# Weights loaded into the place they are converted in, a conversion in four stages, and y stored from one tile: a change to a fused attention and two-layer kernel

## The chip, the cores and the metric

The kernel runs on one core of a Trainium2 chip. The metric is the device time of one execution in microseconds, the median over runs. Before the change it is 770.56 us (three runs, 769.83 to 771.4).

## What is computed

Three layers follow each other, all in float32 (only the weights arrive as float64):

```python
# 1. attention with local masks: 4 batches, 8 heads, 576 positions, head size 64
scores = where(mask, q @ k.T / 8, -1e9)        # plain window 32, or dilated by 4
x = softmax(scores) @ v                        # -> 2304 tokens x 512
# 2. first feed-forward layer
h = x @ w_in                                   # 512 -> 2048
y = (h - tanh(h)) @ w_out                      # 2048 -> 512
# 3. second feed-forward layer
h = y @ w_in2                                  # 512 -> 1024
u = h * softmax(h)
out = ((u - mean(u)) / sqrt(var(u) + 1e-6) * g_ln) @ w_out2   # 1024 -> 512
```

## The kernel before

**Weights.** Every weight matrix is cut into pieces of 128 x 512 values: 16 of `w_in`, 16 of `w_out`, 8 each of `w_in2` and `w_out2`. A piece comes from HBM as raw float64 words, 512 KB (`w_load`, on SP's queue), and is turned into two float32r halves, high and low, by five or six instructions: ScalarE scales the upper word (`a`), VectorE takes the sign (`and`), merges exponent and mantissa in two `scalar_tensor_tensor` steps, ScalarE writes the high half (`hi`, a cast), VectorE subtracts for the low half (`lo`). `w_step` does one such step for several pieces at once: in its stages a piece is new, then merged, then split. In the kernel before, `hi` and the `lo` that reads it stand first in the same call (`w_parts`). Raw words lie in a pool of three buffers, the two halves in pools `wi` and `wo`.

**Phase 1, attention of the first 384 tokens.** Eight units (a pair of heads and a pair of query blocks each) go through a loop of eleven rounds. A round r does the score matmuls of unit r (`qk_f32`), the value matmuls of unit r-3 (`pv_pe`), the transposes of unit r-2 (`tr_pe`), one `w_step` (in rounds 1 to 10), and then on VectorE the masked reduction of unit r (line 163), on ScalarE its four exponentials, on VectorE the reciprocal of the sums of unit r-1, and on GpSimd the normalisation (line 205). At a round's end `load_unit(r + 3)` issues two loads on SP's queue: `qkr` (two buffers) and `v` (four buffers).

**Phase 2, first layer and the rest of the attention.** 96 steps s (6 groups of 384 tokens x 16 pieces) run, each of two slots: `mm1(s)`, twelve matmuls of `h`, and `mm2(s - 5)`, twelve matmuls that add to the four PSUM tiles of `y`. Between them stand the pieces of the 40 other attention units, placed by slot (`plan`), and in the first 42 slots the rest of the `w_step` calls, at a pace set by `WA / WB`. From unit 22 the scores use float32r halves made by `prep_unit`. At a group's last step `mm2` copies the four tiles to SBUF (`ys`) and stores them to HBM (`y_dr`), two at a time through one buffer. In the last group (s = 80 on) the 16 pieces of the second layer are converted, one `w_step` a step, and `y` is read back (`yr`).

**Phase 3, second layer.** 18 blocks of 128 tokens, with `mm3`, `trz` and `mm4`.

Each engine works through its instructions in program order, and so does SP's queue of DMA issues: a wait there holds back all that is behind it. A buffer that is handed out again makes its new writer wait for all readers of the old content, also where those stand later in the program.

Of the kernel before, what the change touches and what calls it, by code (L numbers as in the profile page):

```python
# [7 lines left out]
F32 = mybir.dt.float32  # L8
F32R = mybir.dt.float32r
I32 = mybir.dt.int32  # L10
AF = mybir.ActivationFunctionType
ALU = mybir.AluOpType
# [3 lines left out]
B, H, S, D = 4, 8, 576, 64  # L16
# [3 lines left out]
G = 384  # L20
NG = NTOK // G
NQ, NK = 96, 128
NU = 8
QC, KC = 4 * NQ, 4 * NK
KD = DM // 128
NF = FF // 128
NF2 = FF2 // 128
# [1 line left out]
NT = NTOK // TT  # L29
YT = 256  # L30
LAG = 5
WA, WB = 24, 40
SW = range(1, 11)
W0 = 11

# [2 lines left out]
def tile_kernel(ctx: ExitStack, tc: tile.TileContext, qk, vw, cst, w_in, w_out, w_in2, w_out2, g_ln, out):  # L38
    nc = tc.nc
    ctx.enter_context(tc.manual_schedule())  # L40

    const = ctx.enter_context(tc.tile_pool(name="const", bufs=1, side="left"))
    wi_p = ctx.enter_context(tc.tile_pool(name="wi", bufs=NF, side="left"))
    wo_p = tc.alloc_tile_pool(name="wo", bufs=NF, side="left")
    raw_p = tc.alloc_tile_pool(name="raw", bufs=3, side="left")
    qs_p = None
    g_p = ctx.enter_context(tc.tile_pool(name="g", bufs=2, side="right"))
    x_p = ctx.enter_context(tc.tile_pool(name="x", bufs=2, side="right"))
    at_p = tc.alloc_tile_pool(name="at", bufs=2, side="right")
# [19 lines left out]

    wq, wld, wa, wf = [], [], [], []

    def w_load():
        if wq:
            lst, c, pool, src, tag, nm = wq.pop(0)
            raw = raw_p.tile([128, 1024], I32, tag="raw", name="raw_" + nm)
            nc.sync.dma_start(out=raw, in_=src)
            wld.append((lst, c, pool, tag, nm, raw.rearrange("p (n t) -> p n t", t=2)))

    def w_parts():
        if wf:
            lst, c, pool, tag, nm, f = wf.pop(0)
            w = pool.tile([128, 2, 512], F32R, tag=tag, name=nm)
            nc.scalar.copy(out=w[:, 0], in_=f)
            nc.vector.tensor_tensor(out=w[:, 1], in0=f, in1=w[:, 0].bitcast(F32), op=ALU.subtract)
            lst[c] = w

    def w_step():

        w_parts()
        new = wld.pop(0) if wld else None
        if new:
            lst, c, pool, tag, nm, r = new
            a = raw_p.tile([128, 512], F32, tag="wa", name="wa_" + nm, bufs=2)
            y = raw_p.tile([128, 512], I32, tag="wy", name="wy_" + nm, bufs=3)
            nc.scalar.activation(out=a, in_=r[:, :, 1].bitcast(F32), func=AF.Copy, scale=2.0 ** -112)
            nc.vector.tensor_scalar(out=y, in0=r[:, :, 1], scalar1=-2 ** 31, scalar2=None, op0=ALU.bitwise_and)
        if wa:
            *e, ao, yo = wa.pop(0)  # L100
            nc.vector.scalar_tensor_tensor(out=yo, in0=ao.bitcast(I32), scalar=3, in1=yo,
                                           op0=ALU.logical_shift_left, op1=ALU.bitwise_or)
            wf.append((*e, yo.bitcast(F32)))
        if new:
            nc.vector.scalar_tensor_tensor(out=y, in0=r[:, :, 0], scalar=29, in1=y,  # L105
                                           op0=ALU.logical_shift_right, op1=ALU.bitwise_or)
            wa.append((lst, c, pool, tag, nm, a, y))
        w_load()

    wi, wo = [None] * NF, [None] * NF  # L110

    for c in range(NF + LAG):
        if c < NF:
            wq.append((wi, c, wi_p, w_in[c], "wi", f"wi{c}"))
        if c >= LAG:
            wq.append((wo, c - LAG, wo_p, w_out[c - LAG], "wo", f"wo{c - LAG}"))

# [3 lines left out]
    def load_unit(u):  # L123
        if u < NU * NG:
            r = at_p.tile([128, QC + KC], F32, tag="qkr", name=f"qkr{u}")
            n = 64 if u < NFU else 128
            nc.sync.dma_start(out=r[:n], in_=qk[u, :n])
            v = at_p.tile([NK, 2, 2, D], F32, tag="v", name=f"v{u}", bufs=4)
            nc.sync.dma_start(out=v.rearrange("p b h d -> p (b h d)"), in_=vw[u])
            un[u] = dict(r=r, v=v)  # L130

    def prep_unit(u):
        if not NFU <= u < NU * NG:
            return []
        r = un[u]["r"]
        s = qs_p.tile([128, QC + 2 * KC], F32R, tag="qks", name=f"qks{u}")
        un[u]["s"] = s
        return [
            lambda: nc.vector.tensor_copy(out=s[:, 0:QC + KC], in_=r),
            lambda: nc.vector.tensor_tensor(out=s[64:128, 0:QC], in0=r[64:128, 0:QC],  # L140
                                            in1=s[64:128, 0:QC].bitcast(F32), op=ALU.subtract),
            lambda: nc.vector.tensor_tensor(out=s[:, QC + KC:], in0=r[:, QC:],
                                            in1=s[:, QC:QC + KC].bitcast(F32), op=ALU.subtract),
        ]
# [106 lines left out]
    load_unit(1)  # L251
    w_load()
    load_unit(2)
    w_load()
    back = None
    for r in range(NU + 3):
        t = qk_f32(r, st_ps, "qk") if r < NU else None
# [26 lines left out]
    ghl, yb = {}, {}  # L284
# [3 lines left out]
    def at(slot, fn):  # L288
        later.setdefault(slot, []).append(fn)
# [28 lines left out]
    def mm2(s):  # L318
        g, c = divmod(s, NF)
        gs = ghl.pop(s)  # L320
        if c == 0:
            yb[g] = [y_ps.tile([128, 512], F32, tag=f"y{m}", name=f"y{g}_{m}")[:, 0:G] for m in range(KD)]
        for m in range(KD):
            for i, (a, b) in enumerate(((0, 0), (0, 1), (1, 0))):
                nc.tensor.matmul(yb[g][m], wo[c][:, a, m * 128:(m + 1) * 128], gs[:, b],  # L325
                                 start=(c == 0 and i == 0), stop=(c == NF - 1 and i == 2))
        if c == NF - 1:
            for i in range(0, KD, 2):
                ys = g_p.tile([128, 2, G], F32, tag="ys", name=f"ys{g}_{i}", bufs=1)
                nc.vector.tensor_copy(out=ys[:, 0], in_=yb[g][i])  # L330
                nc.scalar.copy(out=ys[:, 1], in_=yb[g][i + 1])
                nc.scalar.dma_start(out=y_dr[:, i:i + 2, g * G:(g + 1) * G], in_=ys)

    u0, u1 = NU, NU * NG
    preps = []
# [4 lines left out]
    def plan():  # L340


        ready = 0
        for u in range(u0, u1 + 2):
            p = 4 * u - 41 if u >= 2 * NU else (2, 6, 8, 12, 14, 16, 18, 20)[u - u0]
            q = p + 2 if u >= 2 * NU or u < u0 + 4 else p + 1
            if u < u1:
                at(p, lambda u=u: preps.extend(prep_unit(u + 1)))
                for i in range(3):
                    at(p + i, lambda: preps.pop(0)() if preps else None)  # L350
                if u < NFU:
                    piece(p, lambda u=u: qk_f32(u, a_ps, "at"))
                    at(p + 1, lambda u=u: sm_exp(u))
                    at(p + 2, lambda u=u: sm_norm(u))
                else:
                    piece(p, lambda u=u: qk_half(u, 0, a_ps, "at"))
                    at(p + 2, lambda u=u: sm_exp(u, (0, 1)))
                    piece(p + 1, lambda u=u: qk_half(u, 1, a_ps, "at"))
                    at(p + 3, lambda u=u: sm_exp(u, (2, 3)))
                    at(p + 4, lambda u=u: sm_norm(u))  # L360
                at(p + 1, lambda u=u: load_unit(u + 2))
            if u0 <= u - 1 < u1:
                piece(q, lambda u=u: tr_pe(u - 1, a_ps, "at"))
            if u0 <= u - 2 < u1:
                piece(q + 1, lambda u=u: pv_pe(u - 2, a_ps, "at"))
# [3 lines left out]

    NS = NG * NF  # L370
    w2i, w2o = [None] * (2 * KD), [None] * NF2
    wq2 = [(w2i, 2 * k + n, wi_p, w_in2[k, n], "wi", f"w2i{2 * k + n}") for k in range(KD) for n in range(2)]
    wq2 += [(w2o, j, wi_p, w_out2[j], "wi", f"w2o{j}") for j in range(NF2)]

    yt, y_raw = {}, {}

# [17 lines left out]
    slot = 0  # L394
    done = [len(SW)]
    for s in range(NS + LAG):
        if s == NF + LAG:
            assert not (wq or wld or wa or wf)
            raw_p.release()
            qs_p = tc.alloc_tile_pool(name="qs", bufs=2, side="left", reuse_waits="tile")  # L400
        if s == NS - NF:
            assert not todo and not later and not (wq or wld or wa or wf), (todo, later)
            a_ps.release()
            at_p.release()
            qs_p.release()
            raw_p = tc.alloc_tile_pool(name="raw2", bufs=2, side="left", reuse_waits="tile")
            h2a = tc.alloc_tile_pool(name="h2a", bufs=1, space=PSUM, side="right", reuse_waits="tile")
            p2 = tc.alloc_tile_pool(name="p2", bufs=2, side="right", reuse_waits="tile")
            wq.extend(wq2)
            w_load()  # L410
            w_load()
# [31 lines left out]
            load_y(2)  # L443
    for fn in nxt:
        fn()
    while wq or wld or wa or wf:
        w_step()


    raw_p.release()  # L450
    wo_p.release()
    h_ps.release()
    y_ps.release()
# [182 lines left out]
```

## Time and profile before

| | |
|---|---|
| time, median of 3 runs | 770.56 us |
| profiled execution, its own time | 771.82 us |
| its span, first to last instruction | 770.0 us |
| TensorE busy | 729.4 us, 95% |
| VectorE, ScalarE, GpSimd busy | 470.0, 367.1, 132.3 us |
| mean granted TensorE clock | 0.989 |

Times inside the profile are counted from the span's start. A busy TensorE is not one at its peak: the same twelve matmuls take 2.1 to 4.2 us in different places. A bracket behind an instruction of the timeline tells how long its engine had been idle before it, and what ended that.

### The profile page before, as it was taken

Reading aid. Unit: us, or ns where it says so; the run is one execution under the profiler, and the core shown is the slowest. Engines: PE = TensorE matmul, PEld = TensorE weight load, DVE = VectorE, ACT = ScalarE, POOL = GpSimd, SP = SyncE. Lnnn points to the kernel's source line nnn. Section 1 sums busy time; section 2 is a strip of 40 time slices with the busy share of each in tenths; the row PEclk is TensorE's granted clock in tenths of the full one; section 3 lists DMA queues with packets and bytes.
Section 4 is the critical chain, followed back from the end, with each engine's and each line's share of the span. In section 5 each row is a group of like instructions: output and inputs, shape, how many; then the busy total and the mean of one; then the engine's idle time right before and its main releaser. Section 6 shows DMA issues by size and latency. Waiting matters only on the chain.

```text
span 770.0 us, 11751 instructions
## 1 busy us (share of the span) xinstructions
PE 729.4 (95%) x4168; PEld 657.8 (85%) x4168; DVE 470.0 (61%) x1297; ACT 367.1 (48%) x1015; POOL 132.3 (17%) x187
## 2 busy tenths in 40 slices
PE   5658899999999999999999999799999999999998
PEld 4547789999999899989998999799888888888885
DVE  4688788746665766666666535498365555555453
ACT  4656666644443544444444434345145544445454
POOL 1210322111111111111111100010133123231210
PEclk9999899999999999999999999899999999999999
DMA  7565354222222222121212102434201011110001
GB/s 188 180 215 154 110 187 162 92 70 77 63 62 78 88 63 63 62 89 55 64 61 94 63 1 82 155 133 138 68 1 56 29 40 56 42 54 28 14 28 42
DMA packets 30283, 63.62 MB, mean 83 GB/s; under 512 B 3088, under 2 KB 16912, under 8 KB 30224
## 3 DMA queue, kind: packets, MB, share of 16 engines
q1 hardware_dynamic: 26960, 58.15, 23.6%
q10 hardware_dynamic: 3264, 4.72, 1.7%
q8 instruction: 33, 0.54, 0.3%
q14 instruction: 26, 0.21, 0.1%
HBM read 53.42 MB, written 9.44 MB: 82 GB/s over the span
## 4 chain that ended last, share of the span: by engine, by line
PE 88%; DMA 4%; DVE 3%; ACT 2%; issue 1%; POOL 1%; SPq 0%; ACTq 0%; POOLq 0%; DVEq 0%
PE y L325 27%; PE h L298 25%; PE po L529 13%; PE h L467 13%; PE pv L233 3%; PE zt L510 2%; DMA raw_wi<-in_w_in_dram 2%; PE qkp L158 2%; PE tp L212 2%; PE qkp L178 2%; ACT p L198 1%; DMA y_dr<-ys 1%; POOL p L205 1%; DVE wy_wi L105 1%; DMA raw_wo<-in_w_out_dram 0%
## 5 line engine op out<-in xcount | busy, mean ns | idle before, releaser
L298 PE MATMUL h<-x,wi 128*128 128x384 f32 x1152 | 225.3, 346 | 3.3 <-DVE x L244 2.0
L325 PE MATMUL y<-gs,wo 128*128 128x384 f32 x1152 | 222.6, 343 | 4.3 <-DVE ys L330 4.3
L325 PEld LDWEIGHTS y<-gs,wo 128*128 128x128 f32 x1152 | 199.9, 190 | 9.4 <-DVE ys L330 4.6
L298 PEld LDWEIGHTS h<-x,wi 128*128 128x128 f32 x1152 | 202.0, 193 | 5.5 <-DVE x L244 2.3
L205 POOL TENSOR_TENSOR p<-p,rs 96x512 f32<-96x512 f32 x48 | 77.9, 1623 | 368.0 <-DVE rs L204 315.3
L306 ACT ACTIVATE t<-h 128x384 f32<-128x384 f32 x96 | 46.9, 489 | 125.3 <-PE h L298 119.3
L467 PE MATMUL h<-w2i,yt 128*128 128x512 f32 x432 | 104.9, 397 | 0.0
L529 PE MATMUL po<-w2o,z 128*128 128x512 f32 x432 | 104.1, 396 | 0.1
L529 PEld LDWEIGHTS po<-w2o,z 128*128 128x128 f32 x432 | 80.7, 188 | 20.4 <-ACT z L518 1.9
L518 ACT ACTIVATE z<-zt,gl_sb 128x128 fp32r<-128x128 f32 x144 | 51.0, 367 | 96.9 <-PE zt L510 48.6
L467 PEld LDWEIGHTS h<-w2i,yt 128*128 128x128 f32 x432 | 79.7, 187 | 18.4
L198 ACT ACTIVATE p<-p,nm 96x128 f32<-96x128 f32 x192 | 75.0, 393 | 36.3 <-DVE nm L163 36.3
L519 DVE SCALAR_TENSOR_TENSOR z<-zt,gl_sb,z 128x128 fp32r<-128x128 f32 x144 | 48.9, 350 | 69.2 <-ACT z L518 69.2
L312 ACT CAST gs<-t 128x384 fp32r<-128x384 f32 x96 | 49.1, 511 | 54.0 <-DVE t L309 53.7
L244 DVE TENSOR_TENSOR x<-pv,x 128x192 fp32r<-128x192 f32 x48 | 20.5, 428 | 77.1 <-ACT x L243 77.1
L309 DVE TENSOR_TENSOR t<-h,t 128x384 f32<-128x384 f32 x96 | 52.9, 551 | 23.0 <-ACT t L306 22.9
L315 DVE TENSOR_TENSOR gs<-t,gs 128x384 fp32r<-128x384 f32 x96 | 56.1, 585 | 9.8 <-ACT gs L312 9.7
L233 PE MATMUL pv<-pt,v 128*64 128x96 f32 x384 | 29.7, 281 | 15.7 <-ACT pt L218 9.1
L233 PEld LDWEIGHTS pv<-pt,v 128*64 128x64 f32 x384 | 19.8, 151 | 28.6 <-issue 12.4
L158 PE MATMUL qkp<-qkr 64*96 64x128 f32 x176 | 31.6, 334 | 8.2 <-DMA qkr<-in_qk_dram 7.6
L387 POOL TENSOR_TENSOR yt<-yr,yt 128x1024 fp32r<-128x1024 f32 x9 | 21.9, 2430 | 93.9 <-DMA raw_w2o<-in_w_out_dram 62.3
L158 PEld LDWEIGHTS qkp<-qkr 64*96 64x96 f32 x176 | 25.9, 201 | 13.0 <-DMA qkr<-in_qk_dram 6.9
(68 smaller groups left out, 708.2 us busy)
## 6 DMA issues: line engine op xcount, KB each, us to landing
qkr<-in_qk_dram SPq DMA_DIRECT2D x26, 448.0 KB, 3.4
raw_wi<-in_w_in_dram SPq DMA_DIRECT2D x16, 512.0 KB, 4.5
raw_wo<-in_w_out_dram SPq DMA_DIRECT2D x16, 512.0 KB, 4.2
v<-in_vw_dram SPq DMA_DIRECT2D x48, 128.0 KB, 2.1
qkr<-in_qk_dram SPq DMA_DIRECT2D x22, 224.0 KB, 4.3
y_dr<-ys ACTq DMA_DIRECT2D x12, 384.0 KB, 2.4
yr<-y_dr SPq DMA_DIRECT2D x9, 512.0 KB, 4.1
out_dram<-o SPq DMA_DIRECT2D x18, 256.0 KB, 2.0
```

The costliest lines, as they stand in the source:

```text
L158: nc.tensor.matmul(ps[:, b], d["r"][:64, b * NQ:(b + 1) * NQ], d["r"][:64, QC + b * NK:QC + (b + 1) * NK], start=True, stop=True)
L198: nc.scalar.activation(out=d["p"][:, b], in_=d["p"][:, b], func=AF.Exp, scale=-1.0, bias=d["nm"][:, b:b + 1], accum_out=d["sm"][:, b:b + 1])
L205: nc.gpsimd.tensor_tensor(out=d["p"], in0=d["p"], in1=d["rs"].unsqueeze(2).to_broadcast([NQ, 4, NK]), op=ALU.mult)
L233: nc.tensor.matmul(ps[64 * h:64 * h + 64, b * NQ:(b + 1) * NQ], d["v"][:, b, h], d["pt"][:, (2 * h + b) * NQ:(2 * h + b + 1) * NQ], start= ...
L298: nc.tensor.matmul(ps, w[:, a, k * 128:(k + 1) * 128], xt[g, k][:, b], start=(n == 0), stop=(n == 3 * KD - 1))
L309: nc.vector.tensor_tensor(out=t, in0=ps, in1=t, op=ALU.subtract)
L312: nc.scalar.copy(out=gs[:, 0], in_=t)
L315: nc.vector.tensor_tensor(out=gs[:, 1], in0=t, in1=gs[:, 0].bitcast(F32), op=ALU.subtract)
L325: nc.tensor.matmul(yb[g][m], wo[c][:, a, m * 128:(m + 1) * 128], gs[:, b], start=(c == 0 and i == 0), stop=(c == NF - 1 and i == 2))
L467: nc.tensor.matmul(ps[:, n * 512:(n + 1) * 512], y[:, a, k, o:o + TT], w2i[2 * k + n][:, b], start=(q == 0), stop=(q == 3 * KD - 1))
L518: nc.scalar.activation(out=z[:, 0, c], in_=pp[n][:, j], func=AF.Copy, scale=gc)
L529: nc.tensor.matmul(po, z[:, a, j], w2o[j][:, b], start=(q == 0), stop=(q == 3 * NF2 - 1))
```

## The change

- `raw` is allocated under the tag of the piece's final place, one tag for each of the 16 places of `wi` and of `wo`; the three raw buffers are gone. The second layer's 16 pieces take the places wi0 to wi15, so their load waits for the last matmul that reads the place.
- Four raw pieces are asked for ahead of the rounds, where there were two.
- `w_step` has one more stage: `lo` of a piece comes one call after its `hi`, and stands first; `a` and `and` of the new piece come before the `hi`. `WA` is 26 for 24.
- `v` has five buffers for four. The float32r scores' tile `qks` has one buffer for two, in another pool, and its three preparing instructions come two slots later (the copy) and two and one later (the subtractions).
- `ys` holds all four tiles; VectorE copies tiles 0 and 2, ScalarE 1 and 3, and one DMA of 768 KB stores them.

```diff
-WA, WB = 24, 40
+WA, WB = 26, 40
...
-    wi_p = ctx.enter_context(tc.tile_pool(name="wi", bufs=NF, side="left"))
-    wo_p = tc.alloc_tile_pool(name="wo", bufs=NF, side="left")
-    raw_p = tc.alloc_tile_pool(name="raw", bufs=3, side="left")
+    cv_p = ctx.enter_context(tc.tile_pool(name="cv", bufs=2, side="left"))
+    wi_p = ctx.enter_context(tc.tile_pool(name="wi", bufs=1, side="left"))
+    wo_p = tc.alloc_tile_pool(name="wo", bufs=1, side="left")
...
-            raw = raw_p.tile([128, 1024], I32, tag="raw", name="raw_" + nm)
+            raw = pool.tile([128, 1024], I32, tag=tag, name="raw_" + nm)
...
-    def w_parts():
+    def w_step():
+
+        if wh:
+            lst, c, w, f = wh.pop(0)
+            nc.vector.tensor_tensor(out=w[:, 1], in0=f, in1=w[:, 0].bitcast(F32), op=ALU.subtract)
+            lst[c] = w
+        new = wld.pop(0) if wld else None
+        if new:
+            *e, r = new
+            a = cv_p.tile([128, 512], F32, tag="wa", name="wa_" + e[-1])
+            y = cv_p.tile([128, 512], I32, tag="wy", name="wy_" + e[-1], bufs=4)
+            nc.scalar.activation(out=a, in_=r[:, :, 1].bitcast(F32), func=AF.Copy, scale=2.0 ** -112)
+            nc.vector.tensor_scalar(out=y, in0=r[:, :, 1], scalar1=-2 ** 31, scalar2=None, op0=ALU.bitwise_and)
         if wf:
             lst, c, pool, tag, nm, f = wf.pop(0)
             w = pool.tile([128, 2, 512], F32R, tag=tag, name=nm)
             nc.scalar.copy(out=w[:, 0], in_=f)
-            nc.vector.tensor_tensor(out=w[:, 1], in0=f, in1=w[:, 0].bitcast(F32), op=ALU.subtract)
-            lst[c] = w
...
+            wh.append((lst, c, w, f))
...
-            v = at_p.tile([NK, 2, 2, D], F32, tag="v", name=f"v{u}", bufs=4)
+            v = at_p.tile([NK, 2, 2, D], F32, tag="v", name=f"v{u}", bufs=5)
...
-        s = qs_p.tile([128, QC + 2 * KC], F32R, tag="qks", name=f"qks{u}")
+        s = at_p.tile([128, QC + 2 * KC], F32R, tag="qks", name=f"qks{u}", bufs=1)
...
     load_unit(2)
-    w_load()
+    for _ in range(3):
+        w_load()
...
-            for i in range(0, KD, 2):
-                ys = g_p.tile([128, 2, G], F32, tag="ys", name=f"ys{g}_{i}", bufs=1)
-                nc.vector.tensor_copy(out=ys[:, 0], in_=yb[g][i])
-                nc.scalar.copy(out=ys[:, 1], in_=yb[g][i + 1])
-                nc.scalar.dma_start(out=y_dr[:, i:i + 2, g * G:(g + 1) * G], in_=ys)
+            ys = g_p.tile([128, KD, G], F32, tag="ys", name=f"ys{g}", bufs=1)
+            for m in range(KD):
+                if m % 2 == 0:
+                    nc.vector.tensor_copy(out=ys[:, m], in_=yb[g][m])
+                else:
+                    nc.scalar.copy(out=ys[:, m], in_=yb[g][m])
+            nc.scalar.dma_start(out=y_dr[:, :, g * G:(g + 1) * G], in_=ys)
...
-                at(p, lambda u=u: preps.extend(prep_unit(u + 1)))
-                for i in range(3):
+                at(p + 2, lambda u=u: preps.extend(prep_unit(u + 1)))
+                for i in (2, 3, 3):
...
-    wq2 = [(w2i, 2 * k + n, wi_p, w_in2[k, n], "wi", f"w2i{2 * k + n}") for k in range(KD) for n in range(2)]
-    wq2 += [(w2o, j, wi_p, w_out2[j], "wi", f"w2o{j}") for j in range(NF2)]
+    wq2 = [(w2i, 2 * k + n, wi_p, w_in2[k, n], f"wi{2 * k + n}", f"w2i{2 * k + n}")
+           for k in range(KD) for n in range(2)]
+    wq2 += [(w2o, j, wi_p, w_out2[j], f"wi{2 * KD + j}", f"w2o{j}") for j in range(NF2)]
```

## Rows read from the trace of the kernel before

**Rows 1.** The page's slices: TensorE's busy tenths in 40 equal parts of the span.

```profile
PE   5658899999999999999999999799999999999998
```

**Rows 2.** Chain that ended last, first 60 us: start us, us, what.

```profile
18.18 4.99 DMA raw_wi<-in_w_in_dram
...
52.88 4.22 PE h L298 x12
```

**Rows 3.** Timeline of rounds 6 and 7: start, us, engine, line, what, [idle before <-releaser].

```profile
32.13 0.62 ACT L85 CAST wi<-wy_wi 128x512 fp32r<-128x512 f32 x1
...
32.78 0.69 DVE L86 TENSOR_TENSOR wi<-wy_wi,wi 128x512 fp32r<-128x512 f32 x1 [1.47 <-ACT wi L85]
...
35.00 0.28 DVE L163 CUSTOM_DVE_ANT_0 p<-qkp,cst_sb 96x128 f32<-96x128 f32 x1
...
36.30 0.17 DVE L204 RECIPROCAL rs<-rs 96x4 f32<-96x4 f32 x1
...
36.65 1.04 POOL L205 TENSOR_TENSOR p<-p,rs 96x512 f32<-96x512 f32 x1 [4.13 <-ACT p L198]
...
40.25 0.28 DVE L163 CUSTOM_DVE_ANT_0 p<-qkp,cst_sb 96x128 f32<-96x128 f32 x1
```

**Rows 4.** Timeline of SP's issues, 5 to 20 us.

```profile
7.56 0.44 SPq L78 DMA_DIRECT2D raw_wi<-in_w_in_dram  x1
9.45 0.47 SPq L127 DMA_DIRECT2D qkr<-in_qk_dram  x1
...
17.75 0.34 SPq L129 DMA_DIRECT2D v<-in_vw_dram  x1
```

**Rows 5.** SP queue's waits, first 53 us: total us, times, longest.

```profile
SPq L129 <- PE pv L233: 21.4, 6, 4.1
```

**Rows 6.** The qkr load issued at 9.45, issue to landing.

```profile
DMA to landing us min/median/max: 4.9/4.9/4.9
```

**Rows 7.** Busy time by stretch: span, engines' busy us, PEclk, DMA share, GB/s.

```profile
2.00:16.00 14.00, 8.39 (x35) 7.19 (x36) 5.87 (x33) 5.92 (x25) 1.32 (x2) 1.00 0.95 249
16.00:52.88 36.88, 21.48 (x128) 16.02 (x126) 26.50 (x93) 24.56 (x77) 7.24 (x7) 1.00 0.56 182
...
80.30:110.25 29.95, 29.81 (x189) 26.70 (x189) 23.83 (x78) 19.46 (x61) 7.77 (x4) 0.92 0.42 139
```

**Rows 8.** VectorE's line 86, 57 to 77 us: busy, mean ns, idle before it.

```profile
L86 DVE TENSOR_TENSOR wi<-wy_wi,wi 128x512 fp32r<-128x512 f32 x2 | 1.4, 694 | 2.4 <-ACT wi L85 2.4
```

**Rows 9.** Timeline around the longest wait of TensorE in phase 2's start.

```profile
76.25 0.66 DVE L86 TENSOR_TENSOR wo<-wy_wo,wo 128x512 fp32r<-128x512 f32 x1
...
76.49 2.85 POOL L205 TENSOR_TENSOR p<-p,rs 96x512 f32<-96x512 f32 x1 [8.21 <-DVE rs L204]
...
79.39 0.90 PE L212 MATMUL tp<-cst_sb,p 96*128 96x96 f32 x4 [4.25 <-POOL p L205]
```

**Rows 10.** Timeline of the second group's store.

```profile
251.09 0.56 DVE L330 COPY ys<-y 128x384 f32<-128x384 f32 x1 [3.04 <-DMA y_dr<-ys]
```

**Rows 11.** Chain behind that store.

```profile
251.48 1.26 issue
```

**Rows 12.** Chain around the fifth group's store.

```profile
480.61 2.08 PE h L298 x12
...
484.27 7.14 DMA y_dr<-ys
...
498.25 2.09 PE y L325 x12
```

**Rows 13.** Landing of the eight raw_w2i loads.

```profile
DMA to landing us min/median/max: 3.0/3.2/4.4
```

**Rows 14.** Timeline in the last group: two of ScalarE's instructions of one step.

```profile
470.69 0.66 ACT L97 ACTIVATE wa_w2i<-raw_w2i 128x512 f32<-128x512 f32 x1
...
474.46 0.49 ACT L306 ACTIVATE t<-h 128x384 f32<-128x384 f32 x1 [2.53 <-PE h L298]
```

**Rows 15.** Timeline of phase 2: VectorE's idle time ahead of line 244.

```profile
242.49 0.36 DVE L244 TENSOR_TENSOR x<-pv,x 128x192 fp32r<-128x192 f32 x1 [2.80 <-ACT x L243]
```

More of the change, by code (lines that the diff above doesn't have):

```diff
@@ L42, in tile_kernel @@
     const = ctx.enter_context(tc.tile_pool(name="const", bufs=1, side="left"))
-    wi_p = ctx.enter_context(tc.tile_pool(name="wi", bufs=NF, side="left"))
-    wo_p = tc.alloc_tile_pool(name="wo", bufs=NF, side="left")
-    raw_p = tc.alloc_tile_pool(name="raw", bufs=3, side="left")
-    qs_p = None
+    cv_p = ctx.enter_context(tc.tile_pool(name="cv", bufs=2, side="left"))
+    wi_p = ctx.enter_context(tc.tile_pool(name="wi", bufs=1, side="left"))
+    wo_p = tc.alloc_tile_pool(name="wo", bufs=1, side="left")
     g_p = ctx.enter_context(tc.tile_pool(name="g", bufs=2, side="right"))
@@ L66, in tile_kernel @@
     gl_sb = const.tile([128, NF2], F32, name="gl_sb")
-    wq, wld, wa, wf = [], [], [], []
+    wq, wld, wa, wf, wh = [], [], [], [], []
     def w_load():
@@ L85, in w_parts @@
             nc.scalar.copy(out=w[:, 0], in_=f)
-            nc.vector.tensor_tensor(out=w[:, 1], in0=f, in1=w[:, 0].bitcast(F32), op=ALU.subtract)
-            lst[c] = w
[L89 to L98, printed above, removed]
+            wh.append((lst, c, w, f))
         if wa:
-            *e, ao, yo = wa.pop(0)
+            *eo, ao, yo = wa.pop(0)
             nc.vector.scalar_tensor_tensor(out=yo, in0=ao.bitcast(I32), scalar=3, in1=yo,
                                            op0=ALU.logical_shift_left, op1=ALU.bitwise_or)
-            wf.append((*e, yo.bitcast(F32)))
+            wf.append((*eo, yo.bitcast(F32)))
         if new:
@@ L106, in w_step @@
                                            op0=ALU.logical_shift_right, op1=ALU.bitwise_or)
-            wa.append((lst, c, pool, tag, nm, a, y))
+            wa.append((*e, a, y))
         w_load()
@@ L113, in tile_kernel @@
         if c < NF:
-            wq.append((wi, c, wi_p, w_in[c], "wi", f"wi{c}"))
+            wq.append((wi, c, wi_p, w_in[c], f"wi{c}", f"wi{c}"))
         if c >= LAG:
-            wq.append((wo, c - LAG, wo_p, w_out[c - LAG], "wo", f"wo{c - LAG}"))
+            wq.append((wo, c - LAG, wo_p, w_out[c - LAG], f"wo{c - LAG}", f"wo{c - LAG}"))
     xt, un = {}, {}
@@ L396, in tile_kernel @@
     for s in range(NS + LAG):
[L397 to L400, printed above, removed]
         if s == NS - NF:
-            assert not todo and not later and not (wq or wld or wa or wf), (todo, later)
+            assert not todo and not later and not (wq or wld or wa or wf or wh), (todo, later)
             a_ps.release()
             at_p.release()
-            qs_p.release()
-            raw_p = tc.alloc_tile_pool(name="raw2", bufs=2, side="left", reuse_waits="tile")
             h2a = tc.alloc_tile_pool(name="h2a", bufs=1, space=PSUM, side="right", reuse_waits="tile")
@@ L445, in tile_kernel @@
         fn()
-    while wq or wld or wa or wf:
+    while wq or wld or wa or wf or wh:
         w_step()
-    raw_p.release()
     wo_p.release()
```

## The prediction

> **What bounds the kernel now.** I read the page's slices first [rows 1]: TensorE is at 5 to 8 tenths in the first five slices (96 us) and at 9 from then on, with one dip near 490 us. So the time can shrink in the start, at the dip, and in waits too short for a slice; between them TensorE sets the pace, and faster work on other engines buys nothing.
>
> The chain of waits through the start shows what sets the pace there. It passes through loads of raw weights [rows 2] and between them through a loop of VectorE and ScalarE, to `mm1(0)` at 52.88. The timeline of one round [rows 3] shows the loop: ScalarE's `hi` at 32.13, VectorE's `lo` after 1.47 us of idling for it, the other three conversion instructions, the reduction at 35.00, then ScalarE's exponentials and the next `hi`. One round is 40.25 - 35.00 = 5.25 us. SP's queue is late too: `v` of a later unit, behind it the next raw piece, wait for value matmuls 21.4 us in all [rows 5], so a raw piece is issued about one round ahead of its use and takes 5 us [rows 2].
>
> Beyond 80 us TensorE is busy 29.81 of 29.95 us [rows 7]. What stops it later are the stores of `y`: the second half of a store waits for the first half's DMA.
>
> **The change, part by part.**
>
> *Rounds (start to `mm1(0)`).* In rounds 1 to 10 `lo` no longer waits for a `hi` of the same call. VectorE's own round, from `lo` at 32.78 to the end of the reciprocal at 36.47, is 3.7 us [rows 3]; the other engines have less to do in it. The fifth `v` buffer lets SP run one round further ahead, and a raw piece is asked for four rounds ahead of its use. So the round falls from 5.25 to about 3.7 us.
>
> Against that: the DMA engines are full from 2 to 16 us (share 0.95, 249 GB/s, or 243 KB/us) [rows 7], and raw pieces 2 and 3 now go ahead of the `qkr` of unit 3, which SP issued right after raw piece 1 [rows 4]. Ahead of and with that `qkr` stood 4 x 224 + 3 x 128 + 256 + 2 x 512 = 2560 KB; from 2.0 us at 243 KB/us that ends at 12.5, and it landed at 9.45 + 4.9 = 14.35 [rows 4, 6], 1.8 later. With 1024 KB more it lands at 18.6, and unit 3's reduction comes two microseconds later, at 20.6 (about 19.5 before, one round and more behind its matmuls). Four rounds of 3.7 put unit 7's reduction at 35.4, for 40.25.
>
> The tail from there: 1.5 us to the end of the reciprocal (35.00 to 36.47), 2.2 of conversion (32.78 to 35.00), 0.6 of reciprocal and x, then the last normalisation, and 3.2 for transposes (0.9, as in [rows 9]), their copy (0.5), the value matmuls (0.9) and the two instructions for x (0.5 and 0.4). The normalisation took 1.04 us where VectorE idled behind the reciprocal [rows 3], and 2.85 where a `lo` had started 0.24 us ahead of it [rows 9]: it then ended only after the whole group of conversion instructions. In the changed rounds a `lo` stands right behind each reciprocal, so I take 2.85 plus 0.3 of issue: 1.5 + 2.2 + 0.6 + 3.15 + 3.2 = 10.7, `mm1(0)` at 46.1 for 52.88, a gain of 6.8. With 1.04 it would be 8.6.
>
> The Trainium skill, SBUF — State Buffer, "Who interferes with whom", says that a VectorE instruction with two SBUF inputs contends with a GpSimd instruction that reads SBUF, and that the second to issue blocks fully. It speaks against this change; the trace agrees in these two rows (1.04 and 2.85), and the sum above already goes by the row.
>
> In rounds 4 to 7 the blocked normalisation stays hidden: the transposes of unit r-2 come a whole round of score and value matmuls later. Bounds of this part: if DMA moves only the 182 GB/s of the later rounds [rows 7] (178 KB/us), a round of 512 + 224 + 128 KB lasts 4.9 us, unit 7's reduction comes at 40.0 and the gain is 2.2; with no delay by the pieces ahead, and a free GpSimd, it is 9.3. I take 6.0, near the middle: a late piece in any of the rounds costs, none gains.
>
> *Slots 0 to 10.* VectorE still decides until TensorE takes over at 80 us. There, line 86 waits 2.4 us for `hi` in the stretch that ends at the normalisation of 76.49 [rows 8]; that wait goes. `WA` of 26 gives the same number of `w_step` calls up to slot 8 (six either way), where the chain leaves VectorE, and one more by slot 10; VectorE has 6 us idle in the 30 after that [rows 7], so the extra 2.2 us are covered, and cost at most themselves if not. Bounds: -0.4 (the extra call's 2.2 us wholly on the path, against the 1.8 that I take) and 2.4; 1.8 is three quarters of the row, since the next wait in line, that for tanh, may keep some of it.
>
> *Stores of y.* In the second group's store VectorE's third copy waits 3.04 us for the DMA of the first half [rows 10]; behind it stand reductions that free a PSUM buffer, and TensorE waits 1.26 us [rows 11]. Groups three and four show the same, 1.25 and 1.26; the first and the last show none. In the fifth group that DMA takes 7.14 us, since `yr` and raw pieces are in flight, and TensorE stops and is slow for a while after (`mm1` of 494.43 took 3.82 us for 2.08). There `mm2` of 498.25 should have come five half-steps of 2.08 after 480.61, at 491.0 [rows 12]: 7.2 us. With one tile no copy waits for a DMA: four copies of 0.5 us end about 2 us after the last matmul, and VectorE's reductions are done well ahead of the matmuls that wait. Gain 3 x 1.26 + 7.2 = 11.0; at worst 9, if the later issue of two copies costs half a microsecond a group. The DMA of 768 KB then has a whole group's time.
>
> *Second layer's weights.* Now a piece's load waits on SP for the last matmul of its place: piece m starts when `mm1(80 + m)` ends, and its `a` on ScalarE is next to wait for it. Behind the waiting issue on SP stand the later pieces and two `yr`, needed four steps later; behind `a` on ScalarE the `hi` of the piece before, the cast of `gs` and the next tanh. Their consumer is `mm1(83 + m)`, which needs the PSUM tile that tanh and the subtraction free, five half-steps of 2.08 (10.4 us) after the load's start. Load 3.2 [rows 13], 0.4 of issue, four ScalarE instructions of 0.49 to 0.66 [rows 3, 14] and VectorE's 0.6: 6.5 us. So 3.9 us are spare, and I cost it at nothing; with a slower load it costs what lies above 7.1 us, in each of up to 15 steps.
>
> *Prepared scores.* The two subtractions (1.25 us) now fall where VectorE idles 2.80 us [rows 15], about 3 us ahead of the score matmuls; no cost, or 1.25 in each of 25 units if that idle time were gone. `v`'s fifth buffer costs nothing beyond the start.
>
> Sum: 6.0 + 1.8 + 11.0 = 18.8. Against the profiled execution (771.82, span 770.0) 753.0; against the median of 770.56, which is 1.3 lower, 751.8.
>
> **Rivals.**
>
> *The start gives nothing.* The early raw pieces make unit 3 late, and the rounds are then bound by DMA or by GpSimd's normalisation, so that all their gain is spent. For it: the share of 0.95 up to 16 us. Against it: after 16 us the share falls to 0.56 [rows 7]. Only the stores and perhaps the slots gain: 770.6 - 11.0 = 759.6, or 757.8 with the slots.
>
> *The fifth store's stall moves.* The raw pieces, the `yr` and the store of 768 KB still meet at about 485, and one that waits on DMA stops TensorE elsewhere, and leaves it slow after. For it: a load took 7.14 there. Against it: 3.9 us spare. It gives back 7.2: 759.
>
> *Slower: the second layer's loads set the pace.* Place: steps 81 to 95. Every load starts only at the end of a matmul group and the chain load, `a`, `hi`, `gs`, tanh, subtraction must close in 10.4 us. Each microsecond of load above 7.1 costs 15 us in all, so with loads of 8.5 it decides (21 lost against 18.8). For it: loads of 5 us in the full start, and the 7.14. Against it: 3.0 to 4.4 in this very stage [rows 13], with two in flight, where now there is one. At 9 us: 770.6 - 18.8 + 28 = 780.
>
> **How the numbers follow.** The forecast 0.75, the start that gives nothing 0.14, the stall that moves 0.06, the slower one 0.04; 0.01 is left for a sum of nothing. The forecast's own range, from its bounds: gains of 2.2 - 0.4 + 9 = 10.8 to 9.3 + 2.4 + 11.2 = 22.9 and a little for slow matmuls that go in the first slots (24.5), thus 746 to 760. The first two rivals lie at its upper end; so 746 to 760 is also the range. Less than 0.2% (1.5 us) cannot be told from no change here: faster 0.95, same 0.01, slower 0.04.
>
> **What would show it.** Right: reductions (line 163) 3.7 to 4 us apart in units 4 to 7, the first of them later than before; normalisations of 2.85 us; `mm1(0)` at 45 to 48; no idle time of the copies of `ys` for a DMA, and steps of 4.16 us through 480 to 500; the raw pieces of the last group issued one step apart. Wrong: `mm1(0)` at 50 or later; TensorE waiting for tanh's PSUM tiles after step 82; VectorE's subtractions ahead of score matmuls that wait.

## The result, and the profile after

The changed kernel takes 751.35 us (median of four runs, 750.7 to 751.79) against 770.47: a ratio of 0.975, interval 0.9733 to 0.9767, or 19.1 us less. The forecast was 751.8. The profiled execution took 751.79 us, its span is 750.0.

TensorE's slices of the changed kernel:

```profile
PE   3977999999999999999999999999999999999997
```

Against [rows 1] the dip near 490 us is gone, and TensorE stays at 9 from the fifth slice on, for the sixth. The chain of waits through the start:

```profile
9.90 8.50 DMA qkr<-in_qk_dram
...
33.33 0.58 DVE wi L85
...
40.41 2.85 POOL p L205
...
47.25 4.07 PE h L299 x12
```

No raw piece is in it up to `mm1(0)`, which starts at 47.25 for 52.88 [rows 2]. The `qkr` of unit 3 is, landing 8.5 us after its issue for 4.9 [rows 6]. A round of the changed kernel in its timeline:

```profile
33.15 0.17 DVE L204 RECIPROCAL rs<-rs 96x4 f32<-96x4 f32 x1
33.25 0.66 DVE L85 TENSOR_TENSOR wi<-wy_wi,wi 128x512 fp32r<-128x512 f32 x1
...
33.50 2.85 POOL L205 TENSOR_TENSOR p<-p,rs 96x512 f32<-96x512 f32 x1 [1.05 <-ACT p L198]
...
35.50 0.29 DVE L163 CUSTOM_DVE_ANT_0 p<-qkp,cst_sb 96x128 f32<-96x128 f32 x1
...
36.40 0.90 PE L212 MATMUL tp<-cst_sb,p 96*128 96x96 f32 x4 [0.21 <-POOL p L205]
36.62 0.16 DVE L203 TENSOR_SCALAR rs<-sm 96x4 f32<-96x4 f32 x1
36.81 0.17 DVE L204 RECIPROCAL rs<-rs 96x4 f32<-96x4 f32 x1
```

From reciprocal to reciprocal it is 36.81 - 33.15 = 3.66 us, where a round was 5.25 [rows 3]. `lo` (line 85) begins 0.10 us after the reciprocal, with no wait, and the normalisation that starts behind it lasts 2.85 us, for 1.04. It costs TensorE 0.21 us here.

The second group's store in its timeline, and TensorE in the chain behind it:

```profile
238.87 0.56 DVE L332 COPY ys<-y 128x384 f32<-128x384 f32 x1 [1.40 <-PE y L326]
239.38 0.48 ACT L334 COPY ys<-y 128x384 f32<-128x384 f32 x1 [4.15 <-PE y L326]
239.91 0.56 DVE L332 COPY ys<-y 128x384 f32<-128x384 f32 x1 [0.48 <-PE y L326]
...
240.43 0.48 ACT L334 COPY ys<-y 128x384 f32<-128x384 f32 x1 [0.57 <-PE y L326]
```

```profile
240.73 2.11 PE h L299 x12
242.84 0.48 PE pv L233 x8
```

Every copy waits for matmuls alone, and the 1.26 us of [rows 11] between the two pieces of TensorE are gone. The stretch of the fifth group's store by its busy times (span, TensorE, weight loads, VectorE, ScalarE, GpSimd, granted clock, DMA share, GB/s), in the kernel before and then in the changed one:

```profile
484.00:500.00 16.00, 11.74 (x52) 11.42 (x51) 7.44 (x15) 6.47 (x14) 0.00 (x0) 0.79 0.50 166
```

```profile
484.00:500.00 16.00, 16.00 (x95) 16.00 (x94) 15.55 (x26) 8.52 (x19) 2.74 (x1) 1.00 0.36 125
```

In the changed kernel TensorE is busy throughout at a granted clock of 1.00 (2.4 GHz). In the kernel before it stopped for 4.26 us, its clock fell to 0.50 (1.2 GHz) while it stood still, and the matmuls behind the stop ran at that; its timeline and the busy times of the stretch:

```profile
492.14 2.29 PE L325 MATMUL y<-gs,wo 128*128 128x384 f32 x6 [4.26 <-DVE ys L330]
```

```profile
491.27:498.10 6.83, 5.96 (x19) 5.96 (x20) 5.54 (x11) 4.57 (x9) 0.00 (x0) 0.50 0.33 106
```

In the changed kernel `mm1(84)` starts at 467.73 and `mm1(87)` at 480.21, three steps of 4.16 us later, where [rows 12] show the stop. The price of the new place shows in the waits of the last group (who waited, total us, times, longest):

```profile
ACT wa_w2i L92 <- DMA raw_w2i<-in_w_in_dram: 16.9, 7, 3.1
```

ScalarE now idles 2.4 us for each piece; none of it reaches TensorE.

Where the 20.0 us of span went, by marks in both traces: 5.6 up to `mm1(0)`, 1.7 from there to `mm2(0)` (25.39 us for 27.12), 1.1 from there to the first store's first copy (159.3 for 167.8 in all), and the remaining 11.5 in the stores behind it.

### The profile page after: what moved, and what is told of

Read it like the earlier page. It is cut to its first block, busy times and chain, and to the rows that moved or that the text cites. A ratio compares the mean times of both kernels' runs of the same rounds, so it can differ in the third digit from the quotient of the medians.

```text
span 750.0 us, 11682 instructions
## 1 busy us (share of the span) xinstructions
PE 722.7 (96%) x4168; PEld 652.2 (87%) x4168; DVE 492.4 (66%) x1297; ACT 366.4 (49%) x1015; POOL 132.8 (18%) x187
## 4 chain that ended last, share of the span: by engine, by line
PE 89%; DVE 4%; DMA 2%; ACT 2%; POOL 1%; SPq 0%; issue 0%; ACTq 0%; POOLq 0%; DVEq 0%
PE y L326 27%; PE h L299 25%; PE po L526 14%; PE h L464 13%; PE pv L233 3%; PE qkp L158 2%; PE zt L507 2%; PE tp L212 2%; DMA qkr<-in_qk_dram 2%; PE qkp L178 2%; POOL p L205 1%; ACT p L198 1%; DVE wi L85 1%; DVE p L163 1%; DMA raw_wo<-in_w_out_dram 0%; DVE gs L316 0%
## 5 line engine op out<-in xcount | busy, mean ns | idle before, releaser
L299 PE MATMUL h<-x,wi 128*128 128x384 f32 x1152 | 223.0, 343 | 2.0 <-DVE x L244 1.5
L326 PE MATMUL y<-gs,wo 128*128 128x384 f32 x1152 | 219.5, 340 | 0.0
L299 PEld LDWEIGHTS h<-x,wi 128*128 128x128 f32 x1152 | 199.9, 191 | 4.1 <-DVE x L244 1.8
L326 PEld LDWEIGHTS y<-gs,wo 128*128 128x128 f32 x1152 | 197.3, 188 | 4.9
L316 DVE TENSOR_TENSOR gs<-t,gs 128x384 fp32r<-128x384 f32 x96 | 75.7, 788 | 20.9 <-ACT gs L313 18.8
L310 DVE TENSOR_TENSOR t<-h,t 128x384 f32<-128x384 f32 x96 | 52.8, 550 | 18.6 <-ACT t L307 18.6
L481 DVE SCALAR_TENSOR_TENSOR u<-h,e 128x1024 f32<-128x1024 f32 x18 | 22.1, 1225 | 23.9 <-ACT e L480 23.9
L198 ACT ACTIVATION_READ_ACCUMULATOR p<-p,nm 96x1 f32 x192 | 36.1, 188 | 0.0
```

Source lines behind the costliest of these rows:

```text
L198: nc.scalar.activation(out=d["p"][:, b], in_=d["p"][:, b], func=AF.Exp, scale=-1.0, bias=d["nm"][:, b:b + 1], accum_out=d["sm"][:, b:b + 1])
L299: nc.tensor.matmul(ps, w[:, a, k * 128:(k + 1) * 128], xt[g, k][:, b], start=(n == 0), stop=(n == 3 * KD - 1))
L310: nc.vector.tensor_tensor(out=t, in0=ps, in1=t, op=ALU.subtract)
L316: nc.vector.tensor_tensor(out=gs[:, 1], in0=t, in1=gs[:, 0].bitcast(F32), op=ALU.subtract)
```

## The experiments

Marks of each profile, in us: the first reduction of unit 7, `mm1(0)`, the first copy of a store, the span. The runs e1 to e4, e5 to e8, e9 and e10, and e11 and e12 each shared a chip and the runs of the kernel before on it, so times of different groups are best compared by their ratios; only e12 stands beside a run of the changed kernel (e11).

```
                         unit 7   mm1(0)   first copy   span    time     ratio to before (interval)
before                   40.25    52.88    167.8        770.0   770.5
changed                  35.50    47.25    159.3        750.0   751.35   0.975  (0.9733 to 0.9767)
e1  store alone          41.27    54.09    172.0        763.1   764.65   0.9928 (0.9914 to 0.9943)
e2  store undone         34.66    46.41    158.6        755.6   757.04   0.9829 (0.9814 to 0.9843)
e3  three stages         40.53    54.59    171.9        762.6   763.49   0.9907 (0.9891 to 0.9924)
e4  two ahead            33.80    44.89    157.1        747.8   749.66   0.9735 (0.9721 to 0.975)
e5  store alone again    41.21    53.83    167.7        758.8   760.46   0.9872 (0.9849 to 0.9895)
e6  WA 26 alone          40.91    53.63    169.5        770.1   771.5    1.002  (1.0008 to 1.0031)
e7  place one later      35.42    47.15    159.1        754.7   755.63   0.9815 (0.9794 to 0.9835)
e8  unit 7 on VectorE    33.62    44.67    156.8        747.5   749.95   0.9743 (0.9724 to 0.9762)
e9  four v buffers       37.03    48.78    161.0        751.8   753.12   0.9779 (0.975  to 0.9809)
e10 e4 and e8            33.51    44.92    156.8        747.6   749.33   0.9731 (0.9706 to 0.9756)
e11 changed again        34.93    46.66    158.9        749.5   751.3    0.975  (0.9737 to 0.9763)
e12 two ahead again      33.75    44.95    157.0        747.8   749.54   0.9733 (0.9719 to 0.9748)
```

**e1 and e5: the store alone.** The kernel before with the new store. The larger `ys` lacks 0.4 KB of room, which e1 finds in the conversion and e5 elsewhere:

```diff
-            for i in range(0, KD, 2):
...
+            ys = g_p.tile([128, KD, G], F32, tag="ys", name=f"ys{g}", bufs=1)
...
+            nc.scalar.dma_start(out=y_dr[:, :, g * G:(g + 1) * G], in_=ys)
# e1
-            y = raw_p.tile([128, 512], I32, tag="wy", name="wy_" + nm, bufs=3)
+            y = raw_p.tile([128, 512], I32, tag="wy", name="wy_" + nm, bufs=2)
# e5
-    nc = bacc.Bacc("TRN2", ..., dynamic_dma_scratch_size=1024)
+    nc = bacc.Bacc("TRN2", ..., dynamic_dma_scratch_size=512)
```

> The kernel before with one part of the change alone: y is stored from one tile by one DMA. (For room, the conversion's integer tile has two buffers for three; its place is free again before it is asked for, so this should cost nothing.) If the stores' waits are what TensorE loses in phase 2: faster by 11 us (three times 1.3 and 7.2), about 759.4, and mm1(0) unmoved at 52.9. Rival, the stall of the fifth group moves, since its raw pieces, yr and the store still meet: only about 4 us, 766.

> The kernel before with y stored through one tile, this time with the conversion's three integer buffers kept (the 0.4 KB that the larger tile lacks come from the scratch that DMAs issued by GpSimd would use, of which there are none). If two buffers instead of three were what made the start of the first such run 4 us longer: mm1(0) at 52.9 again, and 11 us faster than before, 759.4. Rival: the store itself costs 4 us somewhere ahead of its first use, and the time is 764 to 765 again.

e1 gave only 5.4 us, but its first copy comes 4.2 us later than before the change; from there on it gains 11.1 of span. Its two integer buffers are not free. VectorE's timeline, e1 and then e5:

```profile
60.35 0.69 DVE L86 TENSOR_TENSOR wo<-wy_wo,wo 128x512 fp32r<-128x512 f32 x1
61.08 0.43 DVE L98 TENSOR_SCALAR wy_wo<-raw_wo 128x512 int32<-128x512 int32 x1
```

```profile
60.31 0.69 DVE L86 TENSOR_TENSOR wo<-wy_wo,wo 128x512 fp32r<-128x512 f32 x1
60.92 0.42 DVE L98 TENSOR_SCALAR wy_wo<-raw_wo 128x512 int32<-128x512 int32 x1
```

Where `and` writes the buffer that the `lo` just ahead of it reads, it starts 0.73 us after it, for 0.61, though the `lo` is busy for 0.69 us: the overlap of these two neighbours on VectorE is lost, and so in 27 calls (0.69 to 0.73 us apart, for 0.58 to 0.61). That is some 3 us of VectorE (an estimate, 27 times 0.12), and TensorE waits 11.7 us between `mm1(0)` and the first copy, for 7.3 in e5; how the one becomes the other was not followed. With three buffers (e5) the first copy is at 167.7, as before, and the store gives 9.7 us (8.1 to 11.6); its span is 11.2 shorter. So the store alone does what the prediction has for it.

**e2: the store undone.** The changed kernel with the two-tile loop of the kernel before in `mm2`.

> The changed kernel with y stored through two tiles again. If the stores are worth the same here: slower than the changed kernel by 11 us, 762.5, with the copies waiting 2.5 us for a DMA in each group. Rival: the fifth group's 7 us came from loads that ran ahead in the kernel before; in the changed kernel a raw piece starts only when its place is free and yr comes later, so the DMA of the first half lands in 2.4 to 4 us and little of the 7 us returns: 4 to 5 us, 756.

It is 5.7 us slower than the changed kernel, not 11: the rival. The chain of this run:

```profile
239.24 2.44 DMA y_dr<-ys
```

```profile
476.41 2.75 DMA y_dr<-ys
...
481.48 2.36 PE h L299 x12
```

The second group's wait is back as it was. In the fifth group the DMA lands in 2.75 us, for 7.14 [rows 12], and `mm1` at 481.48 is 0.7 us late (six steps of 4.16 from `mm1` at 455.82 give 480.78), for 7.2. In the kernel before, `yr` and raw pieces were in flight at that moment; now a raw piece starts only when its place is free, and `yr` behind them on SP's queue starts at 479.19, when the first half has landed. So the 7.2 us go by the new store alone (e5), and nearly all of them go without it. That it is the new place which does the latter is read from this trace; the place alone, in the kernel before, was not run.

**e3: three stages.** The changed kernel with `lo` behind its `hi` again, both ahead of the new piece:

```diff
     def w_step():
+        if wf:
+            lst, c, pool, tag, nm, f = wf.pop(0)
+            w = pool.tile([128, 2, 512], F32R, tag=tag, name=nm)
+            nc.scalar.copy(out=w[:, 0], in_=f)
+            wh.append((lst, c, w, f))
         if wh:
             lst, c, w, f = wh.pop(0)
             nc.vector.tensor_tensor(out=w[:, 1], in0=f, in1=w[:, 0].bitcast(F32), op=ALU.subtract)
             lst[c] = w
...
-        if wf:
-            lst, c, pool, tag, nm, f = wf.pop(0)
-            w = pool.tile([128, 2, 512], F32R, tag=tag, name=nm)
-            nc.scalar.copy(out=w[:, 0], in_=f)
-            wh.append((lst, c, w, f))
```

> The changed kernel with the low half again in the same call as the high half, ahead of the new piece, as before the change; places, loads ahead, v's buffers and the store stay. If the wait of lo for hi is what made a round 5.2 us: the rounds of units 4 to 7 are 5 to 5.3 us again, and since unit 3 is still late, mm1(0) comes at 53 to 54, later than before the change; some 7 to 8 us slower than the changed kernel, 759. Rival: it was the late loads that made the rounds long; then rounds stay below 4.3 us and the time within 2 us of 751.4.

It is 12.1 us slower than the changed kernel, not 7 to 8. Its rounds, in VectorE's timeline:

```profile
36.74 0.17 DVE L204 RECIPROCAL rs<-rs 96x4 f32<-96x4 f32 x1
38.39 0.69 DVE L90 TENSOR_TENSOR wi<-wy_wi,wi 128x512 fp32r<-128x512 f32 x1 [1.47 <-ACT wi L86]
...
40.53 0.28 DVE L163 CUSTOM_DVE_ANT_0 p<-qkp,cst_sb 96x128 f32<-96x128 f32 x1
```

The wait of 1.47 us [rows 3] is back, and unit 7's reduction comes 5.09 after unit 6's at 35.44. `mm1(0)` is at 54.59, a little beyond the expected 53 to 54; the other 5.3 us, which were not expected, are lost between it and the first copy (117.3 us for 112.05 in the changed kernel). A part of them is TensorE's clock: 10.2 us of that stretch were granted 0.50, for 3.4 us in the changed kernel. The loads that were asked for earlier do nothing for the rounds by themselves.

**e4 and e12: two raw pieces ahead, with e11, the changed kernel beside e12.**

```diff
     load_unit(2)
-    for _ in range(3):
-        w_load()
+    w_load()
```

> The changed kernel with two raw pieces asked for ahead of the rounds, as before the change, for four. If the two extra pieces are what makes unit 3 late: its score matmuls start near 14.5 for 18.5, its reduction near 19 (the third piece lands at 17), rounds stay 3.7 to 3.9 us and mm1(0) comes 1 to 1.5 us earlier than in the changed kernel: 750. Rival: with two pieces ahead the rounds wait for raw pieces again, 5 us each, and the time is 755 to 757.

> The changed kernel once more, on one chip with the next, so that differences of 1 to 2 us can be told: 751.4, ratio 0.975; unit 7's reduction between 34.5 and 35.5, since where the DMA engines are full the same code has come 0.9 us apart.

> Two raw pieces ahead, on the same chip. If the two extra pieces cost what unit 3 waits for: 1.5 to 2 us less than the changed kernel beside it. Rival: the first run's 1.7 us were the spread between chips, and the two agree within 0.5 us.

The score matmuls of unit 3 in e12 and then in e11:

```profile
14.07 1.99 PE L158 MATMUL qkp<-qkr 64*96 64x128 f32 x8
```

```profile
17.95 1.99 PE L158 MATMUL qkp<-qkr 64*96 64x128 f32 x8 [2.79 <-DMA qkr<-in_qk_dram]
```

They start 3.9 us sooner, and `mm1(0)` is at 44.95 for 46.66. Less than half of the 3.9 us arrives, since a raw piece is waited for again, a small part of what the rival had; from e12's chain ahead of `mm1(0)`:

```profile
34.65 5.06 DMA raw_wo<-in_w_out_dram
```

By the times two ahead is 1.7 to 1.8 us below the changed kernel, by the ratios 1.2 to 1.3; on the one chip that they share the intervals overlap (0.9719 to 0.9748, 0.9737 to 0.9763). Two ahead is probably the better version, by 1 to 2 us; the times alone can't confirm it. The changed kernel itself came out as expected (751.3 us, unit 7 at 34.93).

**e6: WA of 26 alone**, in the kernel before (`WA, WB = 26, 40`).

> The kernel before with WA of 26 for 24 alone. If the one more call of the conversion by slot 10 is covered by VectorE's idle time, as the prediction has it: within 1 us of 770.1. Rival: calls that come closer together are on the path while VectorE decides, and it costs 2 to 3 us, as the changed kernel with three stages lost 2.4 us between mm1(0) and the first store against the kernel before.

1.3 us slower (0.6 to 2.4). Some of it lies after `mm1(0)`: 115.9 us to the first copy for 114.9, though 6.8 us of that stretch were granted 0.50, for 10.2 us before. `mm1(0)` itself is 0.75 later though no instruction ahead of it differs, as in e5, so marks of the start can move by that much from run to run. The four-stage conversion needs a denser pace, since each piece takes one call more.

**e7: the place one later.** Each piece of the second layer takes the place after its own.

```diff
-wq2 = [(w2i, 2 * k + n, wi_p, w_in2[k, n], f"wi{2 * k + n}", f"w2i{2 * k + n}")
+wq2 = [(w2i, 2 * k + n, wi_p, w_in2[k, n], f"wi{(2 * k + n + 1) % NF}", f"w2i{2 * k + n}")
...
-wq2 += [(w2o, j, wi_p, w_out2[j], f"wi{2 * KD + j}", f"w2o{j}") for j in range(NF2)]
+wq2 += [(w2o, j, wi_p, w_out2[j], f"wi{(2 * KD + j + 1) % NF}", f"w2o{j}") for j in range(NF2)]
```

> The changed kernel, but each piece of the second layer takes the place after its own, so that its load starts one step (4.16 us) later and mm1(83 + m) comes 6.24 us after the load's start, not 10.4. If the chain load, a, hi, gs, tanh, subtraction is 6.5 us, as the prediction has it: 0.3 us lost in each of 14 steps, 4 us slower than the changed kernel, 755.5; by the changed kernel's trace (subtraction done 6.0 us after the load's start) 0 to 1. Rival, the load does not hang on this chain at all or is hidden: nothing.

4.3 us slower, the expected size, but not in the expected way. Its waits from 455 to 540 us:

```profile
PE y L326 <- DVE ys L332: 2.0, 1, 2.0
PE h L299 <- DVE t L310: 1.6, 2, 1.2
```

Three waits, not fourteen: one where the store's copies stand behind the late conversion, one of 1.25 us where `yr` and a raw piece share the DMA engines (that piece took 4.84 us), and one of 0.38 us where a piece took 3.54 us with nothing beside it and VectorE's `and` 0.79 us for 0.43. In the other steps the chain just fits into 6.24 us. So the load does hang on this chain, the spare 3.9 us of the changed kernel were real, and without them only disturbed steps cost.

**e8: unit 7's normalisation on VectorE.**

```diff
-        nc.gpsimd.tensor_tensor(out=d["p"], in0=d["p"],
...
+        eng = nc.vector if u == NU - 1 else nc.gpsimd
+        eng.tensor_tensor(out=d["p"], in0=d["p"],
...
```

> The changed kernel with the normalisation of unit 7, the last of the rounds, on VectorE for GpSimd (also the line of all other units, which stay on GpSimd). If GpSimd's 2.85 us behind VectorE's conversion are on the path to mm1(0), as the prediction has it: the transposes of unit 7 come 2.5 us earlier, VectorE has 0.6 more to do and then sets the end itself, mm1(0) comes 1.5 to 2 us earlier and the time is 749.6. Rival: VectorE's own work or the raw pieces set mm1(0), and it moves by nothing or 0.6 us later.

749.95 us, as expected, but the interval (0.9724 to 0.9762) holds the changed kernel's ratio too, and the trace gives less: from unit 7's reduction to `mm1(0)` it is 11.05 us for 11.75 (and 11.73 in e11). The chain of the tail:

```profile
38.39 0.69 DVE p L206
39.08 0.60 DVE wi L85
...
43.80 0.83 DVE x L245 x2
44.63 0.04 issue
44.67 4.22 PE h L300 x12
```

GpSimd has left the chain, and VectorE's own work sets the end 0.7 us sooner. The rest of the gain is a unit 7 that came 1.9 us earlier in this profile, ahead of the edit. GpSimd was on the path, for 0.7 us, not 1.5 to 2.

**e9: four buffers for v**, in the changed kernel.

> The changed kernel with four buffers for v, as before the change. If the fifth buffer is what lets SP keep ahead: v of unit u waits for the value matmuls of unit u - 4, one round later, and behind it the scores' load of the next unit is issued some 3 us ahead of its use, for a landing of 4.4; rounds grow by up to 1 us each and the time by 2 to 4 us, 754. Rival: with four raw pieces ahead nothing in SP's queue is urgent, and the time stays within 1 us of 751.4.

753.12 us; the interval (0.975 to 0.9809) reaches the changed kernel. Unit 7's reduction is at 37.03, beyond all five profiles with five buffers and four pieces ahead (33.62 to 35.50), and SP's queue waits for value matmuls, here and then in the changed kernel:

```profile
SPq L129 <- PE pv L233: 19.1, 6, 7.8
```

```profile
SPq L129 <- PE pv L233: 1.5, 5, 0.3
```

With four buffers it is about as much as in [rows 5]. The trace sides with the fifth buffer being worth some 1.5 to 2 us in the start; the times can't confirm it.

**e10: e4 and e8 together.**

> Two raw pieces ahead (749.7 by itself) and unit 7's normalisation on VectorE (749.9 by itself), each some 1.5 us better than the changed kernel. If they act in different stretches, the rounds up to unit 7's reduction and the tail after it: they add, 748.2. Rival: with unit 7 sooner, the last raw pieces or the ramp's DMA set mm1(0), and it is no better than either, 749.7.

749.33 us (0.9706 to 0.9756), no better than e4 or e8: the rival. Its `mm1(0)` is at 44.92, where e4 has 44.89. The traces of e4 and e12 show why: with two pieces ahead VectorE idles 0.2 and 0.6 us for a raw piece, behind the `lo` that follows unit 7's reciprocal; the normalisation beside it takes 1.3 us, for 2.85, and is not in the chain to `mm1(0)`. In e12:

```profile
38.71 1.30 POOL L205 TENSOR_TENSOR p<-p,rs 96x512 f32<-96x512 f32 x1 [0.47 <-DVE rs L204]
```

So the edit of e8 had nothing left to take.

## Why the prediction was right, step by step

**Rounds and tail: 6.0 taken, 5.6 measured.** The late unit 3 was sized to 0.1 us (its matmuls at 18.53 for 18.6), and so was unit 7's reduction (35.50 for 35.4). That these agree so closely is luck: with the same instructions ahead of them, unit 7's reduction stands at 33.62 to 35.50 in five profiles (the changed kernel, e2, e7, e8, e11) and `mm1(0)` at 46.41 to 47.25 in four. The tail is 11.75 us for 10.7. What the sum left out stands in the changed kernel's chain at its end:

```profile
44.68 0.68 ACT wa_wi L92
45.35 0.51 ACT wi L97
45.86 0.41 ACT x L243
```

The two ScalarE instructions of the last call stand ahead of x's cast in program order, 1.2 us that the sum of VectorE, GpSimd and TensorE didn't hold. The 6.0 was chosen between bounds and lay nearer than the sum's own 6.8, partly by luck. (This part's upper bound, 9.3, comes to 9.7 by its own terms, 19.5 + 4 x 3.7 + 8.9 for 52.88; nothing hangs on it.)

**GpSimd.** All six normalisations from 22 us to `mm1(0)` that follow a `lo` take 2.85 to 2.87 us, as the step had it; the trace again agrees with the Trainium skill, SBUF — State Buffer, "Who interferes with whom". In the rounds with score matmuls it costs TensorE 0.2 us, twice, in the tail 0.7 (e8), less than the 1.8 that the sum has between 1.04 and 2.85, because VectorE's work ends almost as late.

**Slots: 1.8 taken, 1.7 up to `mm2(0)`.** Right in size and in kind: the 2.4 us of [rows 8] that VectorE waited for `hi` are gone, and some of them came back as the next wait in line, though not that for tanh but that for the high half of `gs` (VectorE's waits from `mm1(0)` to `mm2(0)`, before and after):

```profile
DVE gs L315 <- ACT gs L312: 0.6, 1, 0.6
```

```profile
DVE gs L316 <- ACT gs L313: 1.7, 2, 1.1
```

The denser pace, costed at nothing, has a price behind `mm2(0)`: by itself about 1.3 us (e6), and 5.3 us are lost up to the first store where it comes without the extra stage (e3). Even so another 1.1 us were gained up to the first store, through TensorE's clock, for which the prediction has only "a little for slow matmuls" at the edge of its range. In the kernel before the clock fell while TensorE stood still for 4.25 us [rows 9], and `mm2(0)` ran at 0.50 (1.2 GHz):

```profile
78.26:85.08 6.82, 5.68 (x25) 5.03 (x25) 5.13 (x19) 4.41 (x15) 3.93 (x2) 0.50 0.11 38
```

It took 3.89 us there, for 2.33 in the changed kernel, where TensorE waits 0.45 us at that place and the clock is 1.00 from `mm2(0)` on.

**Stores: 11.0, measured 11.5 in the changed kernel and 11.2 of span alone (e5).** Right for the kernel before, and the marked 7.2 and 1.26 were what went. The 7.2 us are two things: 4.26 us in which TensorE stood still, and 3.0 us of slow matmuls at a clock of 0.50 behind it (2.29 us for 1.05, and 3.82 for 2.08). The second part varies: in e6, which has the old store too, TensorE stopped for 3.8 us, the clock was back 3.4 us after it fell, for 6.8, and the span behind the first copy is 600.6 us, for 602.2. So some 1.6 of the 11.5 depend on which profile with the old store is taken. But in the changed kernel the store is worth 5.7 (e2): without the new store the fifth group's collision is gone as well, by the trace through the new places, which the prediction did not see; it listed the loads only as a risk. By the Trainium skill, DMA: Bandwidth & Descriptors, "Issuing engines are not separate DMA queues", transfers from different issuing engines share the same DMA engines and interleave; the trace agrees, with a store on ScalarE's queue that took 2.4 us alone and 7.1 beside SP's loads.

**Second layer's weights: nothing, and nothing measured.** The chain that was put at 6.5 us is 6.1. A load starts when `mm1(82)` ends at 461.49; ScalarE's tanh and VectorE's subtraction behind its `a` in the timeline:

```profile
466.49 0.48 ACT L307 ACTIVATE t<-h 128x384 f32<-128x384 f32 x1
...
467.09 0.55 DVE L310 TENSOR_TENSOR t<-h,t 128x384 f32<-128x384 f32 x1
```

The subtraction ends at 467.64. The slower rival had this chain right, and loads of 3.2 to 4.6 us kept it away.

**Prepared scores:** no wait of score matmuls for them in the changed kernel. Only when the second group's DMA waits return (e2) does one appear, 1.1 us in three.

Of the whole 19.1 us, two edits do most of the work: the extra stage (12.1 when undone at the denser pace, e3) and the store (5.7 when undone, 9.7 alone). The store shares the fifth group with the new places; the four pieces ahead probably cost 1 to 2 us. The extra stage alone, in the kernel before, was not run.

## What to carry to other kernels

Where a low part is computed from a high part that another engine writes, put a whole call between them: the wait inside one call was worth more than any buffer here. Prefetch is not free while the DMA engines are full: what is asked for early goes ahead of what is needed first. And a wait that two edits can each remove shows its full price only when one is made alone; undo and add both before dividing a gain. A stop of TensorE can cost more than its own length: of the 7.2 us lost at the fifth store, 3.0 were matmuls at half the clock behind the stop.

## What the runs showed that was not expected

A buffer count that costs no wait in the program's order can still cost time: two integer buffers for three made VectorE start a neighbour 0.12 us later in each call, and the stretch from `mm1(0)` to the first copy 4 us longer (e1 against e5; that the first makes the second is likely, not shown). And the same instructions gave marks far apart from run to run: `mm1(0)` at 52.88, 53.63 and 53.83 in three kernels with the start of before, and unit 7's reduction at 33.62 (e8) and 35.50 with that of the changed kernel. That is as much as the smaller of these edits are worth.
